# Transposing keys as fp32 words of two bf16 elements, with a PSUM copy that separates even and odd elements

## The chip, the cores and the metric

The kernel runs on 1 core of one Trainium2 chip. The metric is device time in microseconds (us). On one core a single execution has no state to compare with, so runs are called fast when they lie within 1.5% of the fastest of the same kernel.

## The reference

Two layers, each run twice with the same weights: grouped-query attention over a key/value cache (decode: one query position per batch), then a gated FFN. Layer norms and residuals are left out below.

```python
B, Sq, D = 4, 1, 512
Hq, Hkv, Sk, Dh = 32, 8, 4096, 128           # 4 query heads share one key/value head
q = (x @ wq).reshape(B, Sq, Hq, Dh)...
scores = jnp.einsum("bhqd,bhkd->bhqk", q, k) * (Dh ** -0.5)
p = _softmax(scores, axis=-1)
o = jnp.einsum("bhqk,bhkd->bhqd", p, v)      # then @ wo, residual
x = x + (_gelu(x @ w_gate) * (x @ w_up)) @ w_down
# ... and once more attention and FFN, with the same k_cache, v_cache and weights
```

All inputs are bf16. The caches are 32 MiB each. The kernel reads the keys once and the values twice, 115.6 MB of DMA in all.

## The kernel before

The score matmuls of this kernel sum over partitions, so they need keys with the 128 elements of a head on partitions. The keys arrive with key positions on partitions. TensorE therefore transposes each block of 128 keys into PSUM (the buffer that matmuls write here), eight blocks to a PSUM tile, and VectorE or ScalarE copies ("evicts") the tile to SBUF (the memory in which the kernel keeps its other tiles). The transposed keys `KT` of one batch are kept for both attention layers.

```python
    ktp = ctx.enter_context(tc.tile_pool(name="ktp", bufs=Hkv))
    kvin = ctx.enter_context(tc.tile_pool(name="kvin", bufs=KV_BUFS))        # 7 buffers of 512 KB
    ps_tp = ctx.enter_context(tc.tile_pool(name="ps_tp", bufs=3, space=bass.MemoryType.PSUM))
    ps_sc = ctx.enter_context(tc.tile_pool(name="ps_sc", bufs=2, space=bass.MemoryType.PSUM))
    # ...
    def evac(out_ap, in_ap):
        evac_ctr[0] += 1
        if evac_ctr[0] % 5 in (1, 3):
            nc.scalar.copy(out=out_ap, in_=in_ap)           # 2 of 5
        else:
            nc.vector.tensor_copy(out=out_ap, in_=in_ap)    # 3 of 5

    def keys(b, kvh):
        kt = ktp.tile([P, C, P], BF16, name="kt", tag="kt")
        KT[kvh] = kt
        for t in range(NT):
            kn = load_kv(A_k_cache, b, kvh, t, "k_t")
            for g in range(CH // TB):
                tp = ps_tp.tile([P, TB, P], BF16, name="tp", tag="tp")
                for i in range(TB):                         # TB = 8
                    nc.tensor.transpose(tp[:, i, :], kn[:, g * TB + i, :], ident_bf[:, :])
                c0 = t * CH + g * TB
                evac(kt[:, c0:c0 + TB, :], tp[:])           # dense on both sides

    def scores(b, g, q_bf):
        sc = ps_sc.tile([P, GH, C, rep], FP32, name="sc", tag="sc")
        for s in range(GH):
            kvh = g * GH + s
            for c in range(C):
                nc.tensor.matmul(sc[:, s, c, :], lhsT=KT[kvh][:, c, :],
                                 rhs=q_bf[:, b, kvh * rep:(kvh + 1) * rep], start=True, stop=True)
        return sc
    # ... softmax: max over keys, shift, exp, sum; values: p times v; FFN
```

In program order, batch `b` runs all its keys and layer-1 attention, then the FFN, then the layer-2 query projection and scores from the kept keys. Batch `b+1` can refill a `kt` buffer only after the layer-2 scores of batch `b` have read it.

Of the kernel before, what the change touches and what calls it, by code (L numbers as in the profile page):

```python
# [8 lines left out]
FP32 = mybir.dt.float32  # L9
BF16 = mybir.dt.bfloat16  # L10
I32 = mybir.dt.int32
ACT = mybir.ActivationFunctionType
# [3 lines left out]
P = 128  # L16
# [3 lines left out]
CH = 16  # L20
TB = 8
GH = 2
# [4 lines left out]
def kernel(  # L27
# [16 lines left out]
    nc = tc.nc  # L44
    B, Sq, D = A_x.shape
    _, Hkv, Sk, Dh = A_k_cache.shape
    HqDh = A_wq.shape[1]
    Hq = HqDh // Dh
    rep = Hq // Hkv
# [4 lines left out]
    C = Sk // P  # L54
    NT = C // CH
    NGRP = Hkv // GH
    assert Hkv % GH == 0 and C % CH == 0 and CH % TB == 0
    assert GH * C * rep * 4 <= 2048 and KF * B * 4 <= 2048 and Hq * B * 4 <= 2048
    scale = float(Dh) ** -0.5

    const = ctx.enter_context(tc.tile_pool(name="const", bufs=1))
    wts = ctx.enter_context(tc.tile_pool(name="wts", bufs=1))
    state = ctx.enter_context(tc.tile_pool(name="state", bufs=1))
    ktp = ctx.enter_context(tc.tile_pool(name="ktp", bufs=Hkv))
    kvin = ctx.enter_context(tc.tile_pool(name="kvin", bufs=KV_BUFS))
    p1p = ctx.enter_context(tc.tile_pool(name="p1p", bufs=3))
    p2p = ctx.enter_context(tc.tile_pool(name="p2p", bufs=NGRP + 1))
    shp = ctx.enter_context(tc.tile_pool(name="shp", bufs=2))
    grp = ctx.enter_context(tc.tile_pool(name="grp", bufs=2 * NGRP))
    small = ctx.enter_context(tc.tile_pool(name="small", bufs=1))  # L70
    ps_tp = ctx.enter_context(tc.tile_pool(name="ps_tp", bufs=3, space=bass.MemoryType.PSUM))
    ps_sc = ctx.enter_context(tc.tile_pool(name="ps_sc", bufs=2, space=bass.MemoryType.PSUM))
    ps_ot = ctx.enter_context(tc.tile_pool(name="ps_ot", bufs=1, space=bass.MemoryType.PSUM))
    ps_misc = ctx.enter_context(tc.tile_pool(name="ps_misc", bufs=2, space=bass.MemoryType.PSUM))

    ident_bf = const.tile([P, P], BF16, name="ident_bf")
    make_identity(nc, ident_bf[:])
    mean_f = const.tile([P, P], FP32, name="mean_f")
    nc.vector.memset(mean_f[:], 1.0 / D)

# [10 lines left out]
    XT = state.tile([P, B, KD], FP32, name="XT")  # L91
    OT_bf = state.tile([P, B, Hq], BF16, name="OT_bf")
    OT2_bf = state.tile([P, B, Hq], BF16, name="OT2_bf")
    q1_bf = state.tile([P, B, Hq], BF16, name="q1_bf")
    q2_bf = state.tile([P, B, Hq], BF16, name="q2_bf")
    xn_bf = state.tile([P, B, KD], BF16, name="xn_bf")

    dq = nc.sync
# [2 lines left out]
    def load_kv(cache, b, kvh, t, name):  # L101
        tl = kvin.tile([P, CH, Dh], BF16, name=name, tag="kv")
        rows = slice(t * CH * P, (t + 1) * CH * P)
        dq.dma_start(out=tl[:], in_=cache[b, kvh, rows].rearrange("(p c) d -> p c d", p=P))
        return tl
# [31 lines left out]
                                    scalar1=mv[:, 0, i:i + 1], scalar2=rstd[:, i:i + 1],  # L137
                                    op0=ALU.subtract, op1=ALU.mult)

    def q_proj(b0, nb, q_bf, parts):  # L140
        bs = slice(b0, b0 + nb)
        hp = Hq // parts
        for part in range(parts):
            qps = ps_misc.tile([P, hp, nb], FP32, name="qps", tag="misc")
            for i in range(hp):
                m = part * hp + i
                for k in range(KD):
                    nc.tensor.matmul(qps[:, i, :], lhsT=wq_sb[:, k, m * Dh:(m + 1) * Dh],  # L148
                                     rhs=xn_bf[:, bs, k], start=(k == 0), stop=(k == KD - 1))
            nc.vector.tensor_copy(  # L150
                out=q_bf[:, bs, part * hp:(part + 1) * hp].rearrange("p b h -> p h b"),
                in_=qps[:])

    def out_proj_add(b0, nb, o_bf):
        bs = slice(b0, b0 + nb)
# [43 lines left out]
    KT = {}  # L199
    evac_ctr = [0]  # L200
# [4 lines that stand above are left out]
            nc.scalar.copy(out=out_ap, in_=in_ap)  # L205
        else:
            nc.vector.tensor_copy(out=out_ap, in_=in_ap)  # L207

    def keys(b, kvh):

        kt = ktp.tile([P, C, P], BF16, name="kt", tag="kt")
        KT[kvh] = kt
        for t in range(NT):
            kn = load_kv(A_k_cache, b, kvh, t, "k_t")
            for g in range(CH // TB):
                tp = ps_tp.tile([P, TB, P], BF16, name="tp", tag="tp")
                for i in range(TB):
                    nc.tensor.transpose(tp[:, i, :], kn[:, g * TB + i, :], ident_bf[:, :])  # L218
                c0 = t * CH + g * TB
                evac(kt[:, c0:c0 + TB, :], tp[:])  # L220

    def scores(b, g, q_bf):
        sc = ps_sc.tile([P, GH, C, rep], FP32, name="sc", tag="sc")
        for s in range(GH):
            kvh = g * GH + s
            for c in range(C):
                nc.tensor.matmul(sc[:, s, c, :], lhsT=KT[kvh][:, c, :],  # L227
                                 rhs=q_bf[:, b, kvh * rep:(kvh + 1) * rep], start=True, stop=True)
        return sc

    def softmax(sc, pool):
        colmax = grp.tile([P, GH, rep], FP32, name="colmax", tag="colmax", bufs=2)
        nc.vector.tensor_reduce(out=colmax[:], in_=sc.rearrange("p s c h -> p s h c"),  # L233
                                axis=AX.X, op=ALU.max)
        gmax = grp.tile([P, GH, rep], FP32, name="gmax", tag="gmax", bufs=2)
        nc.gpsimd.partition_all_reduce(gmax.rearrange("p s h -> p (s h)"),  # L236
                                       colmax.rearrange("p s h -> p (s h)"), P, RED.max)
        sh = shp.tile([P, GH, C, rep], FP32, name="sh", tag="sh")
        nc.vector.tensor_tensor(out=sh[:], in0=sc[:],  # L239
                                in1=gmax[:].unsqueeze(2).broadcast_to([P, GH, C, rep]),  # L240
                                op=ALU.subtract)
        pe = pool.tile([P, GH, C, rep], BF16, name="pe", tag="pe")
        nc.scalar.activation(out=pe[:], in_=sh[:], func=ACT.Exp, scale=scale)  # L243
        ssum = grp.tile([P, GH, rep], FP32, name="ssum", tag="ssum", bufs=2)
        nc.vector.tensor_reduce(out=ssum[:], in_=pe.rearrange("p s c h -> p s h c"),  # L245
                                axis=AX.X, op=ALU.add)
        den = grp.tile([P, GH, rep], FP32, name="den", tag="den", bufs=2)
        nc.gpsimd.partition_all_reduce(den.rearrange("p s h -> p (s h)"),  # L248
                                       ssum.rearrange("p s h -> p (s h)"), P, RED.add)
        rden = grp.tile([P, GH, rep], FP32, name="rden", tag="rden")  # L250
        nc.vector.reciprocal(out=rden[:], in_=den[:])
        return pe, rden

    def values(b, kvh, prob, o_bf):
        pe, rden = prob
        s = kvh % GH
        ot = ps_ot.tile([P, rep], FP32, name="ot", tag="ot")
        for t in range(NT):
            v = load_kv(A_v_cache, b, kvh, t, "v_t")
            for i in range(CH):  # L260
                c = t * CH + i
                nc.tensor.matmul(ot[:], lhsT=v[:, i, :], rhs=pe[:, s, c, :],  # L262
                                 start=(c == 0), stop=(c == C - 1))
        nc.vector.tensor_tensor(out=o_bf[:, b, kvh * rep:(kvh + 1) * rep], in0=ot[:],  # L264
                                in1=rden[:, s], op=ALU.mult)
# [13 lines left out]
    prob2_prev = None  # L279
    for b in range(B):  # L280
        prob1 = {}
        for g in range(NGRP):
            for s in range(GH):
                keys(b, g * GH + s)
            if b == 0 and g == 0:
                dq.dma_start(out=wq_sb[:, :, hq0:], in_=wq_dram[:, :, hq0:])
                q_proj(0, B, q1_bf, NGRP)
            prob1[g] = softmax(scores(b, g, q1_bf), p1p)
            if b == 0 and g == NGRP - 1:
                dq.dma_start(out=wo_sb[:], in_=A_wo.rearrange("(i p) n -> p i n", p=P))  # L290
            if g > 0:
                for s in range(GH):
                    values(b, (g - 1) * GH + s, prob1[g - 1], OT_bf)
        for s in range(GH):
            values(b, (NGRP - 1) * GH + s, prob1[NGRP - 1], OT_bf)
        if b == 0:
            dq.dma_start(out=wg_sb[:], in_=B_w_gate.rearrange("(k p) n -> p k n", p=P))
            dq.dma_start(out=wu_sb[:], in_=B_w_up.rearrange("(k p) n -> p k n", p=P))
            dq.dma_start(out=wd_sb[:], in_=B_w_down.rearrange("(k p) n -> p k n", p=P))
        out_proj_add(b, 1, OT_bf)  # L300
        ffn(b, 1)
        layer_norm(b, 1)
        q_proj(b, 1, q2_bf, 2)
        if prob2_prev is not None:
            for kvh in range(Hkv):
                values(b - 1, kvh, prob2_prev[kvh // GH], OT2_bf)
        prob2_prev = [softmax(scores(b, g, q2_bf), p2p) for g in range(NGRP)]
    for kvh in range(Hkv):
        values(B - 1, kvh, prob2_prev[kvh // GH], OT2_bf)
    out_proj_add(0, B, OT2_bf)  # L310
# [40 lines left out]
```

## Time and profile before

| | before |
|---|---|
| time | 375.66 us median of 2 runs (373.0 to 378.32) |
| profiled span | 377.3 us |
| VectorE (DVE) busy | 137.5 us, 36% |
| ScalarE (ACT) busy | 67.7 us, 18% |
| TensorE matmul busy | 275.4 us, 73% |
| 128 key evictions | 76 on VectorE at 0.687 us, 52 on ScalarE at 1.012 us |

The first lines are from the page of the kernel before: engine busy time with its share of the span, then the busy share in tenths over 40 equal slices for VectorE and for the DMA engines.

```profile
span 377.3 us, 15723 instructions
PE 275.4 (73%) x7268; PEld 263.8 (70%) x7268; DVE 137.5 (36%) x476; ACT 67.7 (18%) x90; POOL 25.0 (7%) x70
...
DVE  0534440032456442333463433334534332351032
...
DMA  7998999999258999947899999758999998579920
```

The DMA row is at 9 over most of the span, so DMA is the first limit. It dips in slices 11 to 13 and around slices 18, 27 and 35: there TensorE works through layer-2 scores and FFN while the seven input buffers are full (from 97 to 122 us the DMA share is 0.52 and TensorE is busy for 24.3 of the 25 us).

The groups of instructions of the kernel before (count, then busy us and mean ns of one, then idle time just before them and what ended it):

```profile
L218 PE MATMUL tp<-ident_bf,k_t 128*128 128x128 bf16 x1024 | 97.2, 271 | 1.2 <-DMA k_t<-in_A_k_cache_dram 0.6
...
L205 ACT COPY kt<-tp 128x1024 bf16<-128x1024 bf16 x52 | 52.6, 1012 | 111.0 <-PE tp L218 93.9
L207 DVE COPY kt<-tp 128x1024 bf16<-128x1024 bf16 x76 | 51.7, 687 | 53.2 <-PE tp L218 51.6
```

Both evicting engines wait for TensorE (`<-PE tp`), not the other way round. The mean of 271 ns is the length of one pipelined transpose; what it costs is its spacing, which the starts in the trace give as 106.7 ns at half clock and 55 to 60 ns at full clock. (The profile lists the clock that TensorE was granted; every record is 0.5 or 1.0 of full speed.)

Three small groups of VectorE come from the same view with shapes kept apart. The second is the batch-strided copy of the query: 32 elements of 2 bytes, written 64 bytes apart. The others write densely.

```profile
L150 DVE CAST q_bf<-qps 128x16 bf16<-128x16 f32 x8 | 1.4, 175 | 14.0 <-PE qps L148 14.0
...
L150 DVE CAST q_bf<-qps 128x32 bf16<-128x32 f32 x4 | 1.0, 290 | 1.2 <-PE qps L148 1.2
...
L116 DVE TENSOR_REDUCE mv<-st 128x8 f32<-128x32 f32 x2 | 0.4, 190 | 1.5 <-PE st L114 1.5
```

### The profile page before, as it was taken

Reading aid. Unit: us, or ns where it says so; the run is one execution under the profiler, and the core shown is the slowest. Engines: PE = TensorE matmul, PEld = TensorE weight load, DVE = VectorE, ACT = ScalarE, POOL = GpSimd, SP = SyncE. Lnnn points to the kernel's source line nnn. Section 1 sums busy time; section 2 is a strip of 40 time slices with the busy share of each in tenths; the row PEclk is TensorE's granted clock in tenths of the full one; section 3 lists DMA queues with packets and bytes.
Section 4 is the critical chain, followed back from the end, with each engine's and each line's share of the span. In section 5 each row is a group of like instructions: output and inputs, shape, how many; then the busy total and the mean of one; then the engine's idle time right before and its main releaser. Section 6 shows DMA issues by size and latency. Waiting matters only on the chain.

```text
span 377.3 us, 15723 instructions
## 1 busy us (share of the span) xinstructions
PE 275.4 (73%) x7268; PEld 263.8 (70%) x7268; DVE 137.5 (36%) x476; ACT 67.7 (18%) x90; POOL 25.0 (7%) x70
## 2 busy tenths in 40 slices
PE   0978872645999897578888885697978866785645
PEld 0878862535998896577788785697978865775545
DVE  0534440032456442333463433334534332351032
ACT  1314230000143330001242230001423400010000
POOL 0000000000112000001100000011010000020000
PEclk9999685555558667555596685555778855555555
DMA  7998999999258999947899999758999998579920
GB/s 283 413 370 271 387 353 382 406 377 394 83 164 269 384 347 347 386 122 220 279 407 406 356 361 410 244 179 241 404 365 349 377 373 302 156 218 347 407 109 4
DMA packets 35762, 115.59 MB, mean 306 GB/s; under 512 B 3176, under 2 KB 9072, under 8 KB 35696
## 3 DMA queue, kind: packets, MB, share of 16 engines
q1 hardware_dynamic: 35696, 114.58, 83.0%
q8 instruction: 57, 0.93, 1.0%
q14 instruction: 9, 0.07, 0.0%
HBM read 114.56 MB, written 0.00 MB: 304 GB/s over the span
## 4 chain that ended last, share of the span: by engine, by line
PE 53%; DMA 16%; DVE 15%; issue 9%; ACT 3%; POOL 3%; SPq 1%; POOLq 0%; ACTq 0%; DVEq 0%
PE tp L218 19%; PE sc L227 14%; DMA v_t<-in_A_v_cache_dram 9%; PE ot L262 7%; DMA wd_sb<-in_B_w_down_dram 6%; PE qps L148 4%; DVE kt L207 2%; PE yT L159 2%; PE hg L170 2%; DVE colmax L233 2%; DMA k_t<-in_A_k_cache_dram 2%; DVE ssum L245 2%; ACT kt L205 2%; ACT pe L243 1%; PE st L114 1%
## 5 line engine op out<-in xcount | busy, mean ns | idle before, releaser
L218 PE MATMUL tp<-ident_bf,k_t 128*128 128x128 bf16 x1024 | 97.2, 271 | 1.2 <-DMA k_t<-in_A_k_cache_dram 0.6
L218 PEld LDWEIGHTS <-k_t 128*128 128x128 bf16 x1024 | 85.2, 125 | 2.0 <-issue 1.0
L262 PE MATMUL ot<-pe,v_t 128*128 128x4 bf16 x2048 | 69.0, 166 | 17.0 <-DMA v_t<-in_A_v_cache_dram 9.7
L262 PEld LDWEIGHTS <-v_t 128*128 128x128 bf16 x2048 | 63.0, 102 | 19.1 <-DMA v_t<-in_A_v_cache_dram 11.0
L227 PE MATMUL sc<-q_bf,kt 128*128 128x4 bf16 x2048 | 69.3, 166 | 9.1 <-DVE kt L207 3.1
L227 PEld LDWEIGHTS <-kt 128*128 128x128 bf16 x2048 | 64.4, 102 | 12.8 <-DVE kt L207 5.3
L205 ACT COPY kt<-tp 128x1024 bf16<-128x1024 bf16 x52 | 52.6, 1012 | 111.0 <-PE tp L218 93.9
L207 DVE COPY kt<-tp 128x1024 bf16<-128x1024 bf16 x76 | 51.7, 687 | 53.2 <-PE tp L218 51.6
L159 PEld LDWEIGHTS <-wo_sb 128*128 128x128 bf16 x640 | 22.4, 102 | 27.8 <-issue 18.6
L159 PE MATMUL yT<-OT_bf,wo_sb 128*128 128x1 bf16 (+1 forms) x640 | 22.2, 165 | 25.5 <-DVE OT_bf L264 16.4
L243 ACT ACTIVATE pe<-sh 128x256 bf16<-128x256 f32 x32 | 13.3, 417 | 99.0 <-DVE sh L239 72.9
L236 POOL PARTITION_ALL_REDUCE gmax<-colmax x32 | 11.8, 369 | 266.6 <-DVE colmax L233 262.0
L264 DVE TENSOR_TENSOR OT_bf<-ot,rden 128x4 bf16<-128x4 f32 x64 | 9.6, 149 | 53.4 <-PE ot L262 53.4
L148 PE MATMUL qps<-xn_bf,wq_sb 128*128 128x1 bf16 (+1 forms) x640 | 18.4, 165 | 8.2 <-DVE xn_bf L136 6.6
L148 PEld LDWEIGHTS <-wq_sb 128*128 128x128 bf16 x640 | 17.9, 104 | 8.8 <-DVE xn_bf L136 7.1
L233 DVE TENSOR_REDUCE colmax<-sc 128x8 f32<-128x256 f32 x32 | 13.6, 424 | 28.0 <-PE sc L227 25.9
L239 DVE TENSOR_TENSOR sh<-sc,gmax 128x256 f32<-128x256 f32 x32 | 13.5, 423 | 11.0 <-POOL gmax L236 10.8
L170 PE MATMUL hg<-xn_bf,wg_sb 128*128 128x1 bf16 (+1 forms) x280 | 8.2, 165 | 10.8 <-DVE xn_bf L136 5.8
L245 DVE TENSOR_REDUCE ssum<-pe 128x8 f32<-128x256 bf16 x32 | 13.3, 415 | 7.5 <-ACT pe L243 7.5
L248 POOL PARTITION_ALL_REDUCE den<-ssum x32 | 13.2, 413 | 39.7 <-DVE ssum L245 39.4
L170 PEld LDWEIGHTS <-wg_sb 128*128 128x128 bf16 x280 | 7.9, 104 | 11.2 <-DVE xn_bf L136 5.0
L194 PEld LDWEIGHTS <-wd_sb 128*128 128x128 bf16 x280 | 8.1, 104 | 8.8 <-issue 5.2
(95 smaller groups left out, 83.1 us busy)
## 6 DMA issues: line engine op xcount, KB each, us to landing
v_t<-in_A_v_cache_dram SPq DMA_DIRECT2D x128, 512.0 KB, 7.1
k_t<-in_A_k_cache_dram SPq DMA_DIRECT2D x64, 512.0 KB, 6.5
wo_sb<-in_A_wo_dram SPq DMA_DIRECT2D x1, 4096.0 KB, 18.8
wq_sb<-in_A_wq_dram SPq DMA_DIRECT2D x1, 3072.0 KB, 15.5
wg_sb<-in_B_w_gate_dram SPq DMA_DIRECT2D x1, 1792.0 KB, 12.3
wu_sb<-in_B_w_up_dram SPq DMA_DIRECT2D x1, 1792.0 KB, 16.3
wd_sb<-in_B_w_down_dram SPq DMA_DIRECT2D x1, 1792.0 KB, 20.9
wq_sb<-in_A_wq_dram SPq DMA_DIRECT2D x1, 1024.0 KB, 5.1
```

The costliest lines, as they stand in the source:

```text
L148: nc.tensor.matmul(qps[:, i, :], lhsT=wq_sb[:, k, m * Dh:(m + 1) * Dh], rhs=xn_bf[:, bs, k], start=(k == 0), stop=(k == KD - 1))
L159: nc.tensor.matmul(yT[:, :, dk], lhsT=wo_sb[:, i, dk * P:(dk + 1) * P], rhs=o_bf[:, bs, i], start=(i == 0 and dk == 0), stop=(i == Hq - 1 ...
L170: nc.tensor.matmul(hg[:, m, :], lhsT=wg_sb[:, k, m * P:(m + 1) * P], rhs=xn_bf[:, bs, k], start=(k == 0), stop=(k == KD - 1))
L205: nc.scalar.copy(out=out_ap, in_=in_ap)
L207: nc.vector.tensor_copy(out=out_ap, in_=in_ap)
L218: nc.tensor.transpose(tp[:, i, :], kn[:, g * TB + i, :], ident_bf[:, :])
L227: nc.tensor.matmul(sc[:, s, c, :], lhsT=KT[kvh][:, c, :], rhs=q_bf[:, b, kvh * rep:(kvh + 1) * rep], start=True, stop=True)
L233: nc.vector.tensor_reduce(out=colmax[:], in_=sc.rearrange("p s c h -> p s h c"), axis=AX.X, op=ALU.max)
L239: nc.vector.tensor_tensor(out=sh[:], in0=sc[:], in1=gmax[:].unsqueeze(2).broadcast_to([P, GH, C, rep]), op=ALU.subtract)
L243: nc.scalar.activation(out=pe[:], in_=sh[:], func=ACT.Exp, scale=scale)
L245: nc.vector.tensor_reduce(out=ssum[:], in_=pe.rearrange("p s c h -> p s h c"), axis=AX.X, op=ALU.add)
L262: nc.tensor.matmul(ot[:], lhsT=v[:, i, :], rhs=pe[:, s, c, :], start=(c == 0), stop=(c == C - 1))
```

## The change

Two neighbouring bf16 elements are taken as one fp32 word, so one fp32 transpose moves two keys per partition: 256 keys instead of 128, and 512 transposes instead of 1024. A transposed word then holds an even element and the odd element beside it, from the same key. The eviction separates them into an even half and an odd half of 128 keys. Each half has the 64 even (or odd) elements of two keys on the 128 partitions, so the query must be split the same way (`q_split`, by small matmuls with a selection matrix), and two score matmuls accumulate. The softmax shift is written back in place in PSUM.

```diff
     def keys(b, kvh):
-        kt = ktp.tile([P, C, P], BF16, name="kt", tag="kt")
+        kt = ktp.tile([P, C // 2, 2, P], BF16, name="kt", tag="kt")
         KT[kvh] = kt
         for t in range(NT):
             kn = load_kv(A_k_cache, b, kvh, t, "k_t")
+            kf = kn.rearrange("p c d -> p (c d)").bitcast(FP32)
             for g in range(CH // TB):
-                tp = ps_tp.tile([P, TB, P], BF16, name="tp", tag="tp")
-                for i in range(TB):
-                    nc.tensor.transpose(tp[:, i, :], kn[:, g * TB + i, :], ident_bf[:, :])
-                c0 = t * CH + g * TB
-                evac(kt[:, c0:c0 + TB, :], tp[:])
+                tp = ps_tp.tile([P, TB // 2, P], FP32, name="tp", tag="tp")
+                for i in range(TB // 2):
+                    u = g * TB // 2 + i
+                    nc.tensor.transpose(tp[:, i, :], kf[:, u * P:(u + 1) * P], ident_f[:, :])
+                u0 = (t * CH + g * TB) // 2
+                evac(kt[:, u0:u0 + TB // 2].rearrange("p u e j -> p u j e"),
+                     tp[:].rearrange("p u j -> p (u j)").bitcast(BF16).rearrange("p (u j e) -> p u j e", j=P, e=2))
...
+            for u in range(C // 2):
+                for e in range(2):
+                    nc.tensor.matmul(sc[:, s, u, :], lhsT=KT[kvh][:, u, e, :],
+                                     rhs=q_bd[:, b, e, kvh].rearrange("p a h -> p (a h)"),
+                                     start=(e == 0), stop=(e == 1))
...
-        sh = shp.tile([P, GH, C, rep], FP32, name="sh", tag="sh")
-        nc.vector.tensor_tensor(out=sh[:], in0=sc[:],
+        nc.vector.tensor_tensor(out=sc, in0=sc,
...
```

The loops of the new eviction run over `u`, then `j`, then `e`. PSUM is read in order; the writes alternate between two places in SBUF that are 128 elements, 256 bytes, apart.

More of the change, by code (lines that the diff above doesn't have):

```diff
@@ L67 @@
     p2p = ctx.enter_context(tc.tile_pool(name="p2p", bufs=NGRP + 1))
-    shp = ctx.enter_context(tc.tile_pool(name="shp", bufs=2))
     grp = ctx.enter_context(tc.tile_pool(name="grp", bufs=2 * NGRP))
@@ L77 @@
     make_identity(nc, ident_bf[:])
+    ident_f = const.tile([P, P], FP32, name="ident_f")
+    nc.vector.tensor_copy(out=ident_f[:], in_=ident_bf[:])
+    half = P // 2
+    sel = const.tile([P, 2, 2, half], BF16, name="sel")
+    for e in range(2):
+        for ab in range(2):
+            nc.vector.tensor_copy(
+                out=sel[:, e, ab], in_=ident_bf[:].rearrange("p (i e) -> p e i", e=2)[:, e])
     mean_f = const.tile([P, P], FP32, name="mean_f")
@@ L93 @@
     OT2_bf = state.tile([P, B, Hq], BF16, name="OT2_bf")
-    q1_bf = state.tile([P, B, Hq], BF16, name="q1_bf")
-    q2_bf = state.tile([P, B, Hq], BF16, name="q2_bf")
+    q1_bf = state.tile([P, Hq, B], BF16, name="q1_bf")
+    q2_bf = state.tile([P, Hq, 1], BF16, name="q2_bf")
+    q1_bd = state.tile([P, B, 2, Hkv, 2, rep], BF16, name="q1_bd")
+    q2_bd = state.tile([P, 1, 2, Hkv, 2, rep], BF16, name="q2_bd")
+    nc.vector.memset(q1_bd[:], 0.0)
+    nc.vector.memset(q2_bd[:], 0.0)
     xn_bf = state.tile([P, B, KD], BF16, name="xn_bf")
@@ L138, in layer_norm, with q_proj @@
                                     op0=ALU.subtract, op1=ALU.mult)
-    def q_proj(b0, nb, q_bf, parts):
+    def q_proj(b0, nb, q_bf, q_bd, parts, d0):
         bs = slice(b0, b0 + nb)
@@ L149, in q_proj, with q_split @@
                                      rhs=xn_bf[:, bs, k], start=(k == 0), stop=(k == KD - 1))
-            nc.vector.tensor_copy(
-                out=q_bf[:, bs, part * hp:(part + 1) * hp].rearrange("p b h -> p h b"),
-                in_=qps[:])
+            nc.vector.tensor_copy(out=q_bf[:, part * hp:(part + 1) * hp, :], in_=qps[:])
+            q_split(d0, nb, q_bf, q_bd, part * hp, hp)
+    def q_split(b0, nb, q_bf, q_bd, h0, hp):
+        bs = slice(b0, b0 + nb)
+        ks = slice(h0 // rep, (h0 + hp) // rep)
+        qe = ps_misc.tile([P, 2, hp, nb], FP32, name="qe", tag="misc")
+        for e in range(2):
+            nc.tensor.matmul(qe[:, e], lhsT=sel[:, e].rearrange("p a i -> p (a i)"),
+                             rhs=q_bf[:, h0:h0 + hp, :], start=True, stop=True)
+        for ab in range(2):
+            pr = slice(ab * half, (ab + 1) * half)
+            for e in range(2):
+                nc.vector.tensor_copy(
+                    out=q_bd[pr, bs, e, ks, ab, :],
+                    in_=qe[pr, e].rearrange("p (k h) b -> p b k h", h=rep))
     def out_proj_add(b0, nb, o_bf):
@@ L214, in keys, with scores @@
             kn = load_kv(A_k_cache, b, kvh, t, "k_t")
+            kf = kn.rearrange("p c d -> p (c d)").bitcast(FP32)
             for g in range(CH // TB):
-                tp = ps_tp.tile([P, TB, P], BF16, name="tp", tag="tp")
-                for i in range(TB):
-                    nc.tensor.transpose(tp[:, i, :], kn[:, g * TB + i, :], ident_bf[:, :])
-                c0 = t * CH + g * TB
-                evac(kt[:, c0:c0 + TB, :], tp[:])
-    def scores(b, g, q_bf):
-        sc = ps_sc.tile([P, GH, C, rep], FP32, name="sc", tag="sc")
+                tp = ps_tp.tile([P, TB // 2, P], FP32, name="tp", tag="tp")
[5 more added lines that the diff above has]
+                     tp[:].rearrange("p u j -> p (u j)").bitcast(BF16).rearrange("p (u j e) -> p u j e", j=P, e=2))
+    def scores(b, g, q_bd):
+        sc = ps_sc.tile([P, GH, C // 2, 2 * rep], FP32, name="sc", tag="sc")
         for s in range(GH):
             kvh = g * GH + s
-            for c in range(C):
-                nc.tensor.matmul(sc[:, s, c, :], lhsT=KT[kvh][:, c, :],
-                                 rhs=q_bf[:, b, kvh * rep:(kvh + 1) * rep], start=True, stop=True)
-        return sc
+            for u in range(C // 2):
+                for e in range(2):
+                    nc.tensor.matmul(sc[:, s, u, :], lhsT=KT[kvh][:, u, e, :],
+                                     rhs=q_bd[:, b, e, kvh].rearrange("p a h -> p (a h)"),
+                                     start=(e == 0), stop=(e == 1))
+        return sc.rearrange("p s u (a h) -> p s (u a) h", a=2)
     def softmax(sc, pool):
@@ L242, in softmax @@
         pe = pool.tile([P, GH, C, rep], BF16, name="pe", tag="pe")
-        nc.scalar.activation(out=pe[:], in_=sh[:], func=ACT.Exp, scale=scale)
+        nc.scalar.activation(out=pe[:], in_=sc, func=ACT.Exp, scale=scale)
         ssum = grp.tile([P, GH, rep], FP32, name="ssum", tag="ssum", bufs=2)
@@ L286 @@
                 dq.dma_start(out=wq_sb[:, :, hq0:], in_=wq_dram[:, :, hq0:])
-                q_proj(0, B, q1_bf, NGRP)
-            prob1[g] = softmax(scores(b, g, q1_bf), p1p)
+                q_proj(0, B, q1_bf, q1_bd, NGRP, 0)
+            prob1[g] = softmax(scores(b, g, q1_bd), p1p)
             if b == 0 and g == NGRP - 1:
@@ L302 @@
         layer_norm(b, 1)
-        q_proj(b, 1, q2_bf, 2)
+        q_proj(b, 1, q2_bf, q2_bd, 2, 0)
         if prob2_prev is not None:
@@ L306 @@
                 values(b - 1, kvh, prob2_prev[kvh // GH], OT2_bf)
-        prob2_prev = [softmax(scores(b, g, q2_bf), p2p) for g in range(NGRP)]
+        prob2_prev = [softmax(scores(0, g, q2_bd), p2p) for g in range(NGRP)]
     for kvh in range(Hkv):
```

## The prediction

> **What bounds it now.** Mostly DMA. The page shows 115.6 MB moved with the DMA engines 83% busy. In the stretch table, while keys are transposed (12 to 54, 122 to 150, 186 to 230, 264 to 309 us) the DMA share is 0.97 to 1.00 at 356 to 386 GB/s, and TensorE, though 80 to 87% busy, only follows. TensorE binds where layer-2 scores mix with the next batch's transposes (97 to 122 us: PE busy 24.3 of 25, DMA 0.52) and in the out-projection/FFN/layer-2 score stretches (about 36 us for batches 1 and 2, DMA 0.7). VectorE is 36% busy. The chain of waits gives transposes 19%, mostly where DMA is saturated anyway.
>
> **What changes.**
> - Transposes: 1024 become 512. In the timeline bf16 transposes start 106.7 ns apart at half clock (58 to 60 at full). [...] the two passes of the layer-norm fp32 matmul end 213 ns apart. [...] My estimate for one fp32 transpose is 110 to 215 ns at half clock, so PE gains 0 to 45 of its 97 us, nearly all where DMA is saturated: at most about 6 us counts (97 to 122 us).
> - Scores: still 2048 matmuls; no change.
> - Query split: per layer-2 projection 4 matmuls and 8 small copies, about 1 to 2 us per batch on the chain.
> - Shift in place in PSUM: neutral.
> - Key eviction decides. Now VectorE takes 687 ns and ScalarE 1012 ns for 1024 bf16, contiguous on both sides. After, the output alternates between two places 256 bytes apart, element by element. [...] Worse, this trace has one scattered 2-byte write: the batch-strided query copy (32 elements, 64 bytes apart) takes 296 ns, where 32 or 56 elements, written contiguously, take 190 and 213. That is about 4.3 ns per element. If the scattered eviction pays this, it takes 2.9 to 4.6 us on VectorE; ScalarE has no such sample.
>
> **Sum.** 76 VectorE evictions. At 1.22 us: 41 us more VectorE, inside about 100 us of VectorE slack in the key stretches (184 us, 82 busy): time about 378. At 2.9 us: 168 more less 100 slack: about 443. At 4.6 us: 297 more, about 570. I give the slow write about 70%.
>
> **Prediction: 495 us, 8 in 10 between 376 and 570. Faster by over 2%: 0.05; within 2%: 0.16; slower: 0.79.**
>
> **What would show it.** Right: the VectorE key copy at 3 to 4.6 us, VectorE busy over 300 us and 65% or more of the span, waits of transposes for the key copies, DMA share in the key stretches well under 0.9, the chain of waits led by VectorE key copies. 512 transposes 110 to 215 ns apart, waiting for free PSUM.
>
> **What would make it wrong.** [...] the copy is 1.2 us and the time stays within 2%; if, besides, the fp32 transpose runs at the bf16 pace, 97 to 122 us shortens and the kernel is a little faster. If an fp32 transpose needs several passes (over 400 ns), TensorE adds 100 us or more and binds instead.

Passages that no trace of this case shows are cut from this text. No term of the sum is cut: it came to about 378 us with a VectorE eviction of 1.22 us, 443 us at 2.9 us and 570 us at 4.6 us. The 1.22 us: the trace of before gives nearly the same as an estimate, about 154 ns for an operation of one element, and (424 less 154) / 256 = 1.05 ns for each element of a 256-element reduction, so 1.23 us for 1024 elements; experiment 2 later measured 1.217 us. The other estimates can be read from that trace too: 110 and 215 ns for an fp32 transpose are close to the 106.7 ns of a bf16 one and to the 213 ns between the two passes of the layer-norm matmul (the trace has 20 records for 10 such matmuls), and "over 400 ns" to twice 213.

## The result, and the profile after

The changed kernel takes 613.15 us (median of 2 runs, 611.28 to 615.03) against 375.66 us. The ratio is 1.632 (95% interval 1.578 to 1.686). Ratios here are the mean time of one kernel's fast runs over that of the other's of the same rounds, so not quite the ratio of the quoted medians. The direction and the mechanism were right; the time lies 43 us beyond the top of the range.

| | before | after |
|---|---|---|
| profiled span, us | 377.3 | 609.5 |
| VectorE busy, us | 137.5 | 435.8 |
| VectorE key eviction, mean us | 0.687 | 4.827 |
| ScalarE key eviction, mean us | 1.012 | 4.736 |
| TensorE transpose spacing at half clock | 106.7 ns per 128 keys | 213 ns per 256 keys |
| score matmul spacing | 26 ns | 26 ns |

The clock records of the changed kernel's run are not to be compared. Its page lists full clock for the first half of the span, yet most fp32 transposes there start 213 ns apart, as they do in the second half where the record says half clock. Where that half records full clock (near 349 us) they start 109 ns apart. So the mean granted clock of 0.748 says little.

The same lines of the page and groups for the changed kernel:

```profile
span 609.5 us, 14841 instructions
PE 317.5 (52%) x6780; PEld 283.9 (47%) x6780; DVE 435.8 (72%) x531; ACT 257.9 (42%) x90; POOL 25.0 (4%) x70
...
DVE  3969898822799989744899787824799797933303
...
DMA  8713439498123554496733345486823535277790
...
DVE 60%; PE 21%; DMA 6%; issue 6%; ACT 5%; POOL 2%; SPq 0%; POOLq 0%; ACTq 0%; DVEq 0%
DVE kt L231 52%; PE sc L255 5%; ACT kt L229 4%; PE ot L290 4%; DMA wd_sb<-in_B_w_down_dram 3%; PE tp L244 3%; DMA v_t<-in_A_v_cache_dram 3%; PE qps L159 3%; PE yT L183 2%; PE yT L218 1%; DVE sc L267 1%; PE hg L194 1%; DVE ssum L273 1%; POOL den L276 1%; DVE colmax L262 1%
...
L231 DVE COPY kt<-tp 128x1024 bf16<-128x1024 bf16 x76 | 349.9, 4827 | 12.7 <-PE tp L244 12.6
L229 ACT COPY kt<-tp 128x1024 bf16<-128x1024 bf16 x52 | 244.5, 4736 | 132.0 <-PE tp L244 114.4
L244 PE MATMUL tp<-ident_f,k_t 128*128 128x128 f32 x512 | 133.9, 427 | 116.7 <-DVE kt L231 54.6
```

The DMA row, once full of nines, is now mostly 1 to 5, and VectorE's row is the full one. The fifth and sixth lines are the chain of waits by engine and by line: VectorE holds 60% of it, its key evictions 52%. The releasers have turned round: TensorE sits idle for 116.7 us before transposes, against 1.2 (54.6 us of it ended by a VectorE eviction, 47.6 us by a ScalarE one, by the list of waits), while VectorE is idle only 12.7 us before its evictions, against 53.2.

Where the time sits shows best by key phase: the stretch of each batch from its first key eviction to its last. These are the stretch tables of both kernels for their four key phases (length, then busy us and count per engine, granted clock, DMA share, GB/s). Before:

```profile
11.70:54.00 42.30, 36.83 (x746) 35.73 (x745) 20.54 (x53) 14.40 (x16) 2.33 (x6) 0.88 0.97 356
98.90:141.80 42.90, 40.00 (x902) 39.07 (x899) 22.35 (x51) 15.66 (x20) 5.32 (x14) 0.65 0.75 259
184.90:221.40 36.50, 32.27 (x704) 30.66 (x701) 17.16 (x35) 14.36 (x16) 2.29 (x6) 0.79 1.00 383
262.50:300.50 38.00, 32.90 (x705) 31.58 (x702) 17.13 (x35) 14.16 (x16) 2.29 (x6) 0.78 0.98 373
sum 159.70, PE 142.00 PEld 137.04 DVE 77.19 ACT 58.59 POOL 12.22; mean PE 35.50 PEld 34.26 DVE 19.30 ACT 14.65 POOL 3.06
```

After:

```profile
11.60:118.60 107.00, 47.05 (x639) 40.16 (x637) 95.96 (x70) 62.00 (x16) 2.33 (x6) 1.00 0.56 198
152.70:252.90 100.20, 48.74 (x795) 42.66 (x791) 93.46 (x53) 62.56 (x20) 5.32 (x14) 1.00 0.39 125
292.70:392.70 100.00, 43.88 (x572) 36.70 (x571) 90.35 (x35) 61.59 (x16) 2.29 (x6) 0.55 0.46 156
433.40:536.10 102.70, 45.36 (x580) 37.95 (x579) 91.98 (x35) 63.24 (x16) 2.29 (x6) 0.50 0.44 150
sum 409.90, PE 185.03 PEld 157.47 DVE 371.75 ACT 249.40 POOL 12.23; mean PE 46.26 PEld 39.37 DVE 92.94 ACT 62.35 POOL 3.06
```

The third busy column is VectorE. The phases grew from 159.7 to 409.9 us, by 250 us; VectorE's work in them grew by 294.6 us and fills 91% of them. Everything outside the phases shrank, from 217.6 to 199.6 us (span less phases). The loss lies in the key phases, and VectorE fills them.

### The profile page after: what moved, and what is told of

Read it like the earlier page. It is cut to its first block, busy times and chain, and to the rows that moved or that the text cites. A ratio compares the mean times of both kernels' runs of the same rounds, so it can differ in the third digit from the quotient of the medians.

```text
span 609.5 us, 14841 instructions
## 1 busy us (share of the span) xinstructions
PE 317.5 (52%) x6780; PEld 283.9 (47%) x6780; DVE 435.8 (72%) x531; ACT 257.9 (42%) x90; POOL 25.0 (4%) x70
## 4 chain that ended last, share of the span: by engine, by line
DVE 60%; PE 21%; DMA 6%; issue 6%; ACT 5%; POOL 2%; SPq 0%; POOLq 0%; ACTq 0%; DVEq 0%
DVE kt L231 52%; PE sc L255 5%; ACT kt L229 4%; PE ot L290 4%; DMA wd_sb<-in_B_w_down_dram 3%; PE tp L244 3%; DMA v_t<-in_A_v_cache_dram 3%; PE qps L159 3%; PE yT L183 2%; PE yT L218 1%; DVE sc L267 1%; PE hg L194 1%; DVE ssum L273 1%; POOL den L276 1%; DVE colmax L262 1%
## 5 line engine op out<-in xcount | busy, mean ns | idle before, releaser
L231 DVE COPY kt<-tp 128x1024 bf16<-128x1024 bf16 x76 | 349.9, 4827 | 12.7 <-PE tp L244 12.6
L229 ACT COPY kt<-tp 128x1024 bf16<-128x1024 bf16 x52 | 244.5, 4736 | 132.0 <-PE tp L244 114.4
L244 PE MATMUL tp<-ident_f,k_t 128*128 128x128 f32 x512 | 133.9, 427 | 116.7 <-DVE kt L231 54.6
L244 PEld LDWEIGHTS tp<-ident_f,k_t 128*128 128x128 f32 x512 | 95.2, 219 | 135.0 <-DVE kt L231 62.7
L255 PE MATMUL sc<-q_bd,kt 128*128 128x8 bf16 x2048 | 73.3, 169 | 94.2 <-DVE kt L231 68.0
L255 PEld LDWEIGHTS <-kt 128*128 128x128 bf16 x2048 | 71.0, 106 | 102.4 <-DVE kt L231 71.1
L271 ACT ACTIVATE pe<-sc 128x256 bf16<-128x256 f32 x32 | 14.2, 452 | 134.0 <-DVE sc L267 112.0
L267 DVE TENSOR_TENSOR sc<-sc,gmax 128x256 f32<-128x256 f32 x32 | 14.8, 465 | 9.2 <-POOL gmax L265 9.0
L279 DVE RECIPROCAL rden<-den 128x8 f32<-128x8 f32 x32 | 7.3, 229 | 9.6 <-POOL den L276 9.6
```

The lines of the kernel that those rows point to most:

```text
L244: nc.tensor.transpose(tp[:, i, :], kf[:, u * P:(u + 1) * P], ident_f[:, :])
L255: nc.tensor.matmul(sc[:, s, u, :], lhsT=KT[kvh][:, u, e, :], rhs=q_bd[:, b, e, kvh].rearrange("p a h -> p (a h)"), start=(e == 0), stop=(e ...
L267: nc.vector.tensor_tensor(out=sc, in0=sc, in1=gmax[:].unsqueeze(2).broadcast_to([P, GH, C, rep]), op=ALU.subtract)
```

## The experiments

The theory: each eviction is slow because its 2-byte elements are written scattered, and the slow evictions bind the key phases. Rivals: the lower speed of a copy that is not dense on both sides, the fp32 transposes, the query split or the held score banks cost as well; a strided read would cost as much as the strided write; the source written as fp32 words is what slows the copy. All kernels passed the check of the result. That check is not sharp: it also passed experiment 3, which puts keys in wrong places.

### 1. The copies measured by themselves

Ten kinds of copy of one PSUM tile, appended to the kernel before:

```diff
+    probe("c0_dense", ...)      # 1024 bf16, dense on both sides
+    probe("c1_read2", ...)      # PSUM read in steps of two, SBUF written densely
+    probe("c2_write_alt", ...)  # PSUM read in order, SBUF written in turn to two places 256 bytes apart
+    probe("c3_alt_sbuf", ...)   # the same from an SBUF source
+    probe("c4_word_alt", ...)   # 512 four-byte words, written in turn to two places
+    probe("c7_write_s2", ...)   # 512 bf16, one every 4 bytes        (also: pairs in turn, words dense,
+    probe("c8_write_s8", ...)   # 256 bf16, one every 16 bytes        words every 16 bytes)
```

> The kernel before, with copies of one PSUM tile appended at its end, three times each on VectorE and on ScalarE (the result stays right). Dense bf16, 1024 elements: 0.69 us on VectorE, 1.01 on ScalarE, as in the key copies before. Theory (a 2-byte element written away from its neighbour is what costs): read in steps of two and written densely, about 1.22 us on VectorE and 1.0 on ScalarE; written alternately to two places 256 bytes apart, 4.6 to 4.9 us on both, also from an SBUF source; pairs of bf16 (a whole word) written alternately, no penalty, about 0.42 us or less for 256 elements; 4-byte words written alternately, about 0.7 us for 512; one 2-byte element every 4 bytes, 512 elements, about 2.3 us. Rival (every change of place costs, whatever the element's width): 512 words written alternately take about 2.3 us, and words 16 bytes apart, 256 of them, about 1.2 us, while one 2-byte element every 4 bytes costs much less than 4 ns each.

From the groups of this kernel, VectorE alone (digits at the end of names are dropped in this view):

```profile
L329 DVE COPY c_write_alt<-tpm 128x1024 bf16<-128x1024 bf16 x3 | 13.7, 4808 | 0.0
...
L329 DVE COPY c_alt_sbuf<-sb_src 128x1024 bf16<-128x1024 bf16 x3 | 7.1, 2629 | 0.0
...
L329 DVE COPY c_read<-tpm 128x1024 bf16<-128x1024 bf16 x3 | 3.6, 1217 | 0.0
L329 DVE COPY c_write_s<-tpm 128x256 bf16<-128x256 bf16 x3 | 3.5, 1431 | 2.0 <-ACT c_write_s L329 2.0
L329 DVE COPY c_word_alt<-tpm 128x512 f32<-128x512 f32 x3 | 2.8, 1050 | 7.1 <-ACT c_write_alt L329 7.1
...
L329 DVE COPY c_dense<-tpm 128x1024 bf16<-128x1024 bf16 x3 | 2.0, 687 | 0.2
L329 DVE COPY c_write_s<-tpm 128x512 bf16<-128x512 bf16 x3 | 1.9, 711 | 1.0 <-ACT c_pair_alt L329 1.0
```

The scattered write costs 4.81 us and the strided read 1.22 us, for the same values. ScalarE is no better with the scattered write: 4.68 to 5.01 us (5.01 is the mean from the SBUF source), and 1.01 us for the strided read. Back to back, the ends of scattered copies stand 4506 ns apart on both engines: 4506 / 1024 = 4.4 ns per element.

My theory in its written form failed on three lines, and the rival on its main ones. One 2-byte element every 4 bytes is cheap (0.71 us for 512, where I expected 2.3); one every 16 bytes is not (1.43 us for 256). Words in turn to two places cost 1.05 us for 512, neither the dense 0.68 nor the rival's 2.3; words 16 bytes apart took 0.60 us for 256, half of the rival's 1.2. Pairs in turn took 0.37 us, as the theory expected. And VectorE from an SBUF source takes 2.63 us, not 4.8. So the cost depends on both the distance and the width; the next measuring kernel (9) settles how.

### 2. Dense writes instead of scattered ones

```diff
-                evac(kt[:, u0:u0 + TB // 2].rearrange("p u e j -> p u j e"),
-                     tp[:]....bitcast(BF16).rearrange("p (u j e) -> p u j e", j=P, e=2))
+                evac(kt[:, u0:u0 + TB // 2],
+                     tp[:]....bitcast(BF16).rearrange("p (u j e) -> p u e j", j=P, e=2))
```

> The changed kernel with the loops of the key copy exchanged: the same values to the same places, but PSUM is read in steps of two elements and SBUF is written densely. Theory (the scattered write is the whole loss): VectorE copy about 1.22 us, ScalarE copy 1.0 us, VectorE busy about 185 us, time 370 to 390 us. Rival ([...] 4-byte transposes 213 ns apart, the query split and the held score banks matter as well): over 400 us. Second rival (a strided read costs as much as a strided write): about 600 us.

Measured: 383.74 us (median of 4), ratio to before 1.018 (1.013 to 1.024).

```profile
L231 DVE COPY kt<-tp 128x1024 bf16<-128x1024 bf16 x76 | 91.4, 1217 | 25.4 <-PE tp L244 24.3
...
L229 ACT COPY kt<-tp 128x1024 bf16<-128x1024 bf16 x52 | 52.6, 1012 | 119.1 <-PE tp L244 102.1
```

Same values, same places, same number of copies; only the order of the loops in the copy's access pattern differs, and 229 of the 237 us are gone. VectorE's copies now take 1.22 us in place of 0.69, and everything else of the change is still there; together that is worth 1.8%, which the record calls unclear at its 2% line.

### 3. The scattered write alone

The kernel before, with bf16 transposes and no other part of the change (keys end up in wrong places):

```diff
-                evac(kt[:, c0:c0 + TB, :], tp[:])
+                evac(kt[:, c0:c0 + TB, :].rearrange("p (u e) j -> p u j e", e=2),
+                     tp[:].rearrange("p i j -> p (i j)").rearrange("p (u j e) -> p u j e", j=P, e=2))
```

> The kernel before with the scattered write alone: bf16 transposes as they were, but the key copy writes alternately to two places 256 bytes apart (keys end up in wrong places, the result is wrong on purpose). Theory: copies of 4.7 to 4.9 us on both engines, VectorE busy about 430 us, key phases about 100 us each as in the changed kernel, time 590 to 615 us, so that the rest of the change is worth under 20 us. Rival (the copy is slow because its source was written as 4-byte words): copies stay under 1.3 us and the time under 400 us.

Measured: 609.83 us (median of 4), ratio 1.620 (1.610 to 1.629).

```profile
L207 DVE COPY kt<-tp 128x1024 bf16<-128x1024 bf16 x76 | 349.6, 4836 | 15.3 <-PE tp L218 13.0
L205 ACT COPY kt<-tp 128x1024 bf16<-128x1024 bf16 x52 | 245.3, 4748 | 125.0 <-PE tp L218 107.8
```

One part of the change, put into the old kernel, makes nearly all of the loss. The rival that blames the fp32 source falls.

### 4. No separation in the copy: a step of two in the score weights

The words stay interleaved in SBUF, the copy is dense on both sides again, and the score matmul takes every second element as its weights:

```diff
-        kt = ktp.tile([P, C // 2, 2, P], BF16, name="kt", tag="kt")
+        kt = ktp.tile([P, C // 2, P, 2], BF16, name="kt", tag="kt")
...
-                    nc.tensor.matmul(sc[:, s, u, :], lhsT=KT[kvh][:, u, e, :],
+                    nc.tensor.matmul(sc[:, s, u, :], lhsT=KT[kvh][:, u, :, e],
```

> The changed kernel with the words left interleaved: the copy is dense on both sides, and the score matmuls load their weights in steps of two elements instead. Theory: VectorE copy back to 0.69 us, ScalarE 1.01 us, time 370 to 385 us if weights in steps of two load as fast as dense ones (score matmuls stay about 27 ns apart). If the stepped load is slower, twice or four times, score matmuls stand 53 or 107 ns apart, TensorE gains 55 or 160 us of work, and the time is about 400 or over 450 us. Since 4-byte transposes stand 213 ns apart, as long as two bf16 transposes at half clock and longer than two at full clock (116 ns), no gain over the kernel before is expected.

Measured: 375.89 us, ratio 0.996 (0.989 to 1.004). With five rounds:

> The version with the step of two in the score weights again, five rounds, to see whether it beats the kernel before: its first runs gave a ratio of 0.996 (0.989 to 1.004). Theory (4-byte transposes stand 213 ns apart at half clock and 108 at full clock, the same time per key as two bf16 transposes at 107 and 57, and the key phases are bound by the DMA anyway): ratio 0.99 to 1.00, the same. Rival (half as many transposes do save time): below 0.985.

Measured: 375.02 us against 377.49 us, ratio 0.992 (0.986 to 0.998).

In these last rounds the record marks three of the eleven runs of the kernel before as slow (380.18 to 380.49 us; 1.5% above the fastest is 380.07). The median of 377.49 us contains them, and the recorded 0.992 comes out only when they are counted. Without them the ratio of the means is 0.995. The ratios of experiments 5 and 6 and of the last run of 7, from the same rounds, would rise by 0.003 to 0.004 too.

Lines of the five-round run:

```profile
L244 PE MATMUL tp<-ident_f,k_t 128*128 128x128 f32 x512 | 96.8, 351 | 1.1 <-ACT kt L229 0.6
...
L231 DVE COPY kt<-tp 128x1024 bf16<-128x1024 bf16 x76 | 51.8, 687 | 47.4 <-PE tp L244 47.2
```

VectorE's copy is back at 0.687 us and score matmuls stay 26 ns apart (68.9 us busy in all, against 69.3 before), so the step in the weights costs nothing here. It is the best version of the change: the same as before within 2%. A gain of 0.8% is not shown, as it rests on the three marginal runs. It also answers what the change could have won. 512 fp32 transposes keep TensorE busy for 96.8 us (100.0 us in the trace of the first run) where 1024 bf16 ones took 97.2. In this trace they start 212 to 215 ns apart at half clock and 108 to 110 at full clock, as long as two bf16 transposes. Halving the count saved no time on TensorE.

### 5. Dense writes, copies dealt evenly

```diff
-        if evac_ctr[0] % 5 in (1, 3):
+        if evac_ctr[0] % 2 == 1:
```

(on top of experiment 2)

> The changed kernel with dense writes (PSUM read in steps of two) and the copies dealt evenly to both engines, since VectorE now takes 1.22 us and ScalarE 1.01 us. Theory (in the 384 us of the unevenly dealt version the slower VectorE copy costs the 8 us over the version with 0.69 us copies): VectorE loses 12 copies of 1.2 us, 376 to 382 us. Rival (the share does not matter): 383 to 385 us.

Measured: 376.19 us, ratio 0.995 (0.989 to 1.002). The 8 us of experiment 2 came from VectorE's larger share of copies that now take 1.22 us.

### 6. The in-place shift alone

The kernel before with the shift written back into the score bank:

> The kernel before with one part of the change alone: the softmax shift written back into the PSUM score bank, and the exponential read from there. Theory: neutral; ScalarE's exponential 385 ns for 417, VectorE's shift 431 for 423, ratio 0.99 to 1.01. Rival (the bank held longer delays the next scores): above 1.01.

Measured: 375.86 us, ratio 0.994 (0.989 to 0.999). Neutral, as predicted.

### 7. Why 613 and not 570: one engine scattered at a time

VectorE scattered, ScalarE dense:

```diff
         if evac_ctr[0] % 5 in (1, 3):
+            o, i = dense          # "(u j e) -> u e j" on the PSUM side
             nc.scalar.copy(out=o, in_=i)
         else:
+            o, i = alt            # the changed kernel's pattern
             nc.vector.tensor_copy(out=o, in_=i)
```

> The changed kernel with ScalarE's key copies exchanged to dense writes (1.0 us each) and VectorE's left scattered (about 4.8 us). Question: why 613 us and not the 570 that the prediction gave for the slowest copy. Theory (VectorE is the bound in the key phases and merely had less slack than I counted): VectorE's work is unchanged, so the time falls little, to 575 to 605 us, by the part of the 38 us of VectorE idle time in the key phases that ScalarE's slow copies cause. Rival (the two slow engines block each other through the three PSUM buffers, and that makes the whole excess): under 570 us. Second rival (ScalarE was the bound): under 500 us.

Measured: 606.66 us, ratio 1.611 (1.600 to 1.623). That is 6.5 us below the changed kernel, a difference not clear of the noise of its two runs, and 2 us outside my expectation's upper end.

```profile
L235 DVE COPY kt<-tp 128x1024 bf16<-128x1024 bf16 x76 | 348.0, 4808 | 12.4 <-PE tp L248 12.2
...
L232 ACT COPY kt<-tp 128x1024 bf16<-128x1024 bf16 x52 | 52.6, 1012 | 258.3 <-PE tp L248 240.9
```

ScalarE's slow copies, 245 us of work, matter almost nothing while VectorE is slow. Both rivals fall.

ScalarE scattered, VectorE dense (the two patterns exchanged):

> The changed kernel with VectorE's key copies exchanged to dense writes (1.22 us each) and ScalarE's left scattered (about 4.7 us). Theory (whichever engine evicts slowest binds the key phases once its work there exceeds the phase): ScalarE has 13 copies a batch, 61 us, above the 38 to 47 us that a key phase takes with fast copies, so phases of 62 to 72 us and a time of 450 to 500 us. Rival (ScalarE's slow copies are off the critical path): 384 to 395 us, as with dense writes on both.

Measured: 544.81 us, ratio 1.448 (1.435 to 1.461): a miss for both theory and rival. The key phases last 80 to 90 us, with ScalarE busy for 61 to 62 us of each:

```profile
11.20:98.00 86.80, 43.17 (x630) 38.87 (x629) 32.63 (x70) 61.53 (x16) 2.33 (x6) 0.55 0.65 226
131.80:221.50 89.70, 46.04 (x771) 41.65 (x768) 32.24 (x53) 62.42 (x20) 5.32 (x14) 0.52 0.42 136
```

Here neither engine is full. My reading: one slow engine that takes every second or third tile in a fixed order holds up the other. The trace fits it, with 84.3 us of idle time before transposes ended by a ScalarE eviction and 116.3 us in which VectorE's evictions wait for transposes; the next run tests one part of it.

The same kernel with a fourth PSUM buffer for transposes (taken from the pool of small results):

```diff
-    ps_tp = ctx.enter_context(tc.tile_pool(name="ps_tp", bufs=3, ...))
+    ps_tp = ctx.enter_context(tc.tile_pool(name="ps_tp", bufs=4, ...))
-    ps_misc = ctx.enter_context(tc.tile_pool(name="ps_misc", bufs=2, ...))
+    ps_misc = ctx.enter_context(tc.tile_pool(name="ps_misc", bufs=1, ...))
```

> The run with scattered writes on ScalarE alone took 545 us where I had expected 450 to 500: its key phases last 80 to 90 us with ScalarE busy for only 61 of them. This is the same kernel with a fourth PSUM buffer for transposes (one taken from the small matmul results). Theory (the copies are dealt out in a fixed order over three buffers, so a ScalarE copy's next transposes, and with them the scores behind them in TensorE's order, wait until the copy three before it has freed its buffer): with four buffers ScalarE waits less, key phases of 65 to 80 us and 490 to 535 us. Rival (ScalarE waits for something else, such as the softmax chain): 540 us or more.

Measured: 526.62 us, ratio 1.393 (1.385 to 1.401), key phases 78 to 84 us. The time is inside the expected range, the phases are a little above theirs. The idle time of transposes ended by a ScalarE eviction fell from 84.3 us to 36.8 us, but the score matmuls' wait for ScalarE evictions rose from 68.6 us to 101.3 us: a part of the wait moved rather than went. The ring of three buffers is part of it, about 18 us of the time; the run also takes a buffer from another pool, and what that cost alone was not measured. The rest of ScalarE's idle time in these phases was not taken apart and stays open.

### 8. Scattered writes, dealt evenly

```diff
-        if evac_ctr[0] % 5 in (1, 3):
+        if evac_ctr[0] % 2 == 1:
```

> The changed kernel with the key copies dealt evenly, 16 a batch to VectorE and 16 to ScalarE in place of 19 and 13; every write still scattered. Theory (VectorE's copies bind): VectorE loses 12 copies of 4.6 us, 55 us, and ScalarE at 16 times 4.7 us, 76 us a batch, stays below it: 550 to 575 us. Rival (something else of the phase binds, such as the shared PSUM buffers or ScalarE): 600 us or more.

Measured: 580.63 us, ratio 1.540 (1.528 to 1.553), 6 us above the expected range and far from the rival. VectorE's work fell by 49 us (386.7 against 435.8) and the time by 32.5 us. So taking work from VectorE does shorten the kernel, but at less than the full rate. That the two engines then hold each other up is argued, not tested; the trace fits it, as the idle time of transposes ended by a ScalarE eviction rose from 47.6 to 121.5 us:

```profile
L248 PE MATMUL tp<-ident_f,k_t 128*128 128x128 f32 x512 | 135.2, 428 | 126.9 <-ACT kt L232 121.5
```

### 9. What a write costs, by step and width

More copies of 256 elements appended to the kernel before: 2-byte elements at steps of 2 to 16 bytes, words at steps of 4 to 16 bytes, in turn to two or four places, and strided reads.

> The kernel before with more copies of one PSUM tile appended: 256 elements each, on both engines, written at steps of 2, 4, 6, 8, 12 and 16 bytes (2-byte elements) and of 4, 8, 12 and 16 bytes (words), in turn to two and to four places 64 bytes apart, and 128 elements read at steps of 2, 4 and 16 bytes. The first row of copies showed 4.4 ns per 2-byte element at 16 bytes, 1.2 ns at 4 bytes, and 1.75 ns per word at 16 bytes. If the cost comes with leaving a line of 16 bytes: at 8 bytes (two elements a line) 2-byte elements take about half of it, 2.2 ns, at 12 bytes about 3.3, at 6 bytes about 1.7 or less, words at 8 bytes about 1.05, at 12 about 1.3; in turn to two or four places 4.4 ns. If it comes with leaving a line of 8 bytes: 4.4 ns at 8, 12 and 16 bytes alike. Reading has no such cost: about 1.04 ns at every step.

From the groups of this kernel, VectorE:

```profile
L329 DVE COPY half_turn_two<-tpm 128x256 bf16<-128x256 bf16 x3 | 3.6, 1433 | 1.6 <-ACT word_step_sixteen L329 1.6
L329 DVE COPY half_step_sixteen<-tpm 128x256 bf16<-128x256 bf16 x3 | 3.5, 1431 | 1.5 <-ACT half_step_twelve L329 1.5
...
L329 DVE COPY half_step_eight<-tpm 128x256 bf16<-128x256 bf16 x3 | 1.9, 757 | 0.2 <-ACT half_step_six L329 0.2
...
L329 DVE COPY word_step_sixteen<-tpm 128x256 f32<-128x256 f32 x3 | 1.5, 601 | 1.2 <-ACT word_step_twelve L329 1.2
...
L329 DVE COPY half_step_four<-tpm 128x256 bf16<-128x256 bf16 x3 | 1.3, 442 | 0.0
...
L329 DVE COPY word_step_eight<-tpm 128x256 f32<-128x256 f32 x3 | 1.1, 418 | 1.0 <-ACT word_step_four L329 1.0
```

Taking the spacing of the ends of back-to-back copies over 256 elements:

| step of the write | 2-byte elements, ns each | 4-byte words, ns each |
|---|---|---|
| 4 bytes | 1.2 (ScalarE) | 1.1 (ScalarE), 1.3 (VectorE) |
| 6 bytes | 1.7 to 1.9 | |
| 8 bytes | 2.2 | 1.1 (ScalarE), 1.3 (VectorE) |
| 12 bytes | 3.3 to 3.6 | 1.3 to 1.4 |
| 16 bytes | 4.4 | 1.75 |
| in turn, 2 or 4 places 64 bytes apart | 4.3 to 4.4 | |

The 2-byte column grows in step with the distance up to 16 bytes, and is the same when every write goes farther: 4.3 to 4.4 ns at 64 bytes here, 4.4 ns at 256 bytes in experiment 1. Words cost VectorE the same at steps of 4 and 8 bytes (417 and 418 ns for 256), and 601 ns at 16. The author's reading is a fixed price for leaving a stretch of 16 bytes: about 4.4 ns where it was filled with 2-byte pieces, and about 1.75 ns where it was filled with whole words. The runs show the cost by step and width; the mechanism behind it was not shown. The expectations of the 16-byte reading held to within 0.3 ns an element, and those of the 8-byte reading did not. All these copies have PSUM as their source; VectorE's copy from SBUF in experiment 1, at 2.2 ns an element (ends 2254 ns apart), does not follow this price, and why is open. Reading PSUM at steps of 4 and 16 bytes cost VectorE the same (285 and 284 ns for 128 elements; 218 ns at a step of 2 bytes, which is dense), so these reads show no such price.

## Why the prediction was right or wrong

- **The deciding step was right.** The scattered key eviction decides; experiments 2 and 3 show it from both sides (383.7 us without it, 609.8 us with it alone). The clue was in the trace of before: a 32-element query copy of 296 ns (290 in the mean of four). At 4.4 ns per element (experiment 1) plus 158 ns for the rest of such an operation, an estimate (175 ns for 16 dense elements, less 16 times the 1.04 ns an element of experiment 2), it should take 299 ns.
- **The signs named beforehand appeared.** VectorE over 300 us busy (436), 72% of the span, transposes waiting for evictions, DMA share in the key phases 0.39 to 0.56, chain of waits led by VectorE's evictions at 52%.
- **The copy's length.** I gave 2.9 to 4.6 us. It is 4.83 us from start to end (4.81 us measured by itself), and 4.60 us of VectorE's time each (349.9 / 76), since neighbours overlap. The high case of the sum was the true one; the central 495 us was a compromise between cases and is where most of the miss from the middle came from.
- **The step that failed, and put the time outside the range: "about 100 us of VectorE slack in the key stretches (184 us, 82 busy)".** VectorE's work grew by 298 us (435.8 less 137.5), as the high case said ("297 more"), but the profiled span grew by 232 us, so only 66 us of slack were found and not 100. Two things were wrong with the 100. The stretches that I had picked were 184 us, but keys are evicted in only 160 us of them, with 82 us of VectorE idle. And of that idle time, the trace of before has about 50 us waiting for transposes, which more evictions can fill; some 28 us is the softmax's own chain (max, gather on GpSimd, shift, exponential, sum), where VectorE waits in program order. After the change, 38 us of idle time are left in the phases, about 23 of them in that chain. So 44 us were absorbed in the phases (294.6 of added work, 250.2 of added length), and about 22 us outside, where the stretches became shorter although VectorE's work there grew slightly; why they did was not taken apart. The size repeats: by the same sum, 64 us were absorbed in experiment 3 and 68 us in experiment 7 with ScalarE dense, so ScalarE's slow copies are not what used up the slack.
- **ScalarE.** I had no sample. Its scattered copies cost the same, 4.74 us, but made dense they save only 6.5 us: next to a slow VectorE they hardly count (first run of experiment 7).
- **TensorE.** "PE gains 0 to 45 of its 97 us": it gained nothing (96.8 and 100.0 us in experiment 4), so the lower end of the estimate held: 213 ns per fp32 transpose against 106.7 ns for a bf16 one, at half clock. How much of that is the weight load and how much the matmul, no run separates. Taking the score weights at a step of two cost nothing: 26 ns between matmuls as before (experiment 4).
- **Score matmuls, query split, shift in place.** Experiment 4 contains all three and is level with before; experiment 6 has the shift alone. For the score matmuls and the shift that was predicted; the 1 to 2 us per batch given for the query split do not show in the time.
- **The copy that is not dense.** The 1.22 us of the low case was measured in experiment 2, where only the read has a step: 1.217 us against 0.687. Less the 154 ns of a one-element operation in the trace of before, that is 1.04 ns an element against 0.52. But its effect, "about 378", came out as 383.7 us.

## What to carry to other kernels

When a copy from PSUM must separate interleaved 2-byte elements, put the step on the read or into the consumer (here, the step of two in the matmul's weights), and write neighbouring elements one after the other; the same values written in another loop order cost 1.2 us instead of 4.8. When costing an access pattern, look for the smallest operation in the trace that already has it: a 32-element copy told what a 1024-element one would do. And idle time of an engine is slack only where the engine waits for work that the change can bring forward; idle time inside a dependent chain that the engine itself serves absorbed little here (28 us before, 23 after).
